# Attention into a mixture of experts on one core: rows of two chunks leave in four transfers of 32 partitions each

## The chip, the core and the metric

The kernel runs on one NeuronCore of a Trainium2 chip. The metric is the device time of one execution in microseconds. A core has a matrix engine (PE, with its weight loads listed as PEld), a vector engine (DVE), a scalar engine (ACT), a general engine (POOL), a queue engine that issues most transfers (SP), and 16 DMA engines that carry them.

## The reference

Eight batches of eight heads go through causal attention with a window of 128 and a linear bias. The result, 4608 rows of 512 numbers, is routed: each row goes to the one of eight experts with the largest gate logit, and its output is scaled with the gate's probability.

```python
scores = scale * np.matmul(q, k.transpose(0, 1, 3, 2))           # q, k, v: (8, 8, 576, 64)
mask = (rel >= 0) & (rel < window)                               # window 128
attn = np.exp(scores - max); attn = attn / (attn.sum(-1) + 1e-9)
x = np.matmul(attn, v).transpose(0, 2, 1, 3).reshape(4608, 512)
logits = x @ w_gate                                              # 8 experts
out[mask] = gate_w[mask, None] * (np.maximum(xe @ w1[e], 0.0) @ w2[e])   # per expert e, F = 1024
```

## The kernel before

**Attention.** The 4608 rows are cut into 36 chunks of 128 (`make_chunks`): per two batches, four chunks of the first, one mixed chunk with the last 64 rows of both ("tail"), and four of the second. Each chunk goes through named steps. `S` are the score matmuls, `F` the masking fold and the row maximum (DVE, L194 and L197), `E` the exponentials (ACT, L203), `T` and `C` turn the probabilities, `P` masks them on POOL, `A` multiplies with v on PE (L242), `X` copies the result, transposed, out of PSUM (ACT, L331), `Y` turns it back into rows on DVE (L334) and calls `store_rows`, which writes the rows to a DRAM buffer `xd`. `I` makes the inverse row sums and stores them beside the rows ("tails", L1322). `G`, `M`, `B`, `L` make the gate logits: PE (L250), a copy on DVE (L350), PE (L257), DVE (L261). The steps `I` and `G` to `L` run once for a batch of one or two chunks (`BATCHES`).

**What sets the order.** A table, `WHEN`, gives each step a time in chunks. During attention the order on all five engines is the one written by hand from this table. Every engine takes its instructions strictly in that order, so an instruction that waits holds up all behind it on its engine.

**Buffers.** `Y` writes into two tiles `x_sb` in turn, one chunk each, so that `Y` of a chunk has to wait until the stores of the chunk two before have landed. `X` writes into `xT`, a tile for two chunks, two such tiles in turn.

**The stores.** `store_rows` issues four transfers for a chunk on SP's queue (L1318). Each takes 32 rows: the source is all 128 partitions of a quarter of `x_sb`, the destination has an outermost dimension of 4 (the quarter of a row), then 32 rows, then 128 numbers (512 bytes). In `xd` a row has four quarters of `SUB` = 128 + `TAIL` numbers, 136 here: 544 bytes.

**SP's queue.** The loads of q (L79, L81), k (L67), v (L90) and the experts' weights (L810, L1060), the row stores, the tails and the gates all stand in this one queue. Its transfers take eight completion counters in turn (`DMAHW0` to `DMAHW7`), and an issue first waits until the transfer that last used its counter, eight places before in the queue, has landed.

**The experts.** From 256 us on, expert by expert, POOL gathers rows of `xd` (L721, L756), they are turned and split into a high and a low part (`xh`, `xl`), and PE runs two layers of three matmuls each on such parts of 4-byte numbers (`first_layer`, L777, and `layer2`, L982). The first 256 rows of the first expert have operands of their own, `e_xh` and `e_xl`, and start while attention still runs.

**Where tiles lie.** Tiles stand one after the other in each partition's memory. By the sizes of the tiles before them, `wh`, `wl` (the split weights), `e_hh`, `e_hl`, `w_raw`, k, q and v start 192 bytes behind a multiple of 512, `xh`, `xl`, `hh` and `hl` 160 bytes behind one, and `e_xh` and `e_xl` on one.

Of the kernel before, what the change touches and what calls it, by code (L numbers as in the profile page):

```python
# [10 lines left out]
F32 = mybir.dt.float32  # L11
# [9 lines left out]
B, H, S, D = 8, 8, 576, 64  # L21
N, DM, E, F = B * S, H * D, 8, 1024
QB = 32
NP = H // 2
GW = 32
TAIL = 8
SUB = 128 + TAIL
# [10 lines left out]
def attention(ctx, tc, st, qT, qE, kT, v, c1, cb, gw, load_c2, logits, chunk_done, store_rows, store_tails, chunks, begun):  # L38
# [5 lines left out]
    ptp = ctx.enter_context(tc.tile_pool(name="a_pt", bufs=2))  # L44
    xp = ctx.enter_context(tc.tile_pool(name="a_x", bufs=2))
    ps_s = ctx.enter_context(tc.tile_pool(name="ps_s", bufs=1, space=PSUM))
# [55 lines left out]
    warm = const.tile([128, 512], BF16, name="warm")  # L102
    nc.vector.memset(warm, 0.0)

    def clear_scores():
# [9 lines left out]

    rows_sb = [const.tile([128, 4, 128], F32, name=f"x_sb{k}") for k in range(2)]
    tails = [const.tile([128, 4, NP * BMAX + TAIL - NP], F32, name=f"tl_sb{k}") for k in range(3)]
# [14 lines left out]
    nc.sync.dma_start(out=c1_sb, in_=c1)  # L132
    first = const.tile([128, 1], F32, name="first")
    nc.vector.memset(first, 0.0)
# [111 lines left out]

    def gates(xT, nb):
        g_ps = ps_r.tile([128, 512], F32, name="g_ps")
        for p in range(NP):
            nc.tensor.matmul(out=g_ps[GW * p:GW * p + GW, 0:128 * nb], lhsT=gw_sb[:, p, :], rhs=xT[:, p, 0:128 * nb],  # L250
                             start=True, stop=True)
        return g_ps

    def turn_gates(lT, nb):
        st["r_ps"] = r_ps = ps_r.tile([128, 512], F32, name="r_ps")
        for j in range(nb):
            nc.tensor.transpose(out=r_ps[:, 128 * j:128 * j + 128], in_=lT[:, 128 * j:128 * j + 128], identity=ident)  # L257
        return r_ps

    def scale_logits(r_ps, tl, dst, nb):  # L260
        nc.vector.tensor_tensor(  # L261
            out=dst.rearrange("q b p c e -> q (b p) c e"),
            in0=r_ps[:, 0:128 * nb].rearrange("q (x y) -> q x y", y=GW)[:, :, 0:2 * E].rearrange("q x (c e) -> q x c e", c=2),
            in1=tl.rearrange("q (c a) x -> q x c a", c=2)[:, 0:NP * nb, :, 0:1].to_broadcast([128, NP * nb, 2, E]), op=ALU.mult)

    ahead = {}
# [27 lines left out]
    def do(op, ch):  # L294
# [33 lines left out]
        elif op == "X":  # L328
            if j == 0:
                tiles["xT", c0] = xp.tile([128, NP, 128 * BMAX], F32, name="xT", bufs=2)  # L330
            nc.scalar.copy(out=every("xT")[:, :, 128 * j:128 * j + 128], in_=tiles.pop(("x", ch)))  # L331
        elif op == "Y":
            rows_sb.append(rows_sb.pop(0))
            keep(tc, nc.vector.transpose(  # L334
                out=rows_sb[-1].rearrange("p s (n j) -> p s n j", j=32),
                in_=every("xT")[:, :, 128 * j:128 * j + 128].rearrange("p n (s i) -> p s n i", i=32)))
            store_rows(ch, subs, rows_sb[-1])
        elif op == "I":
            tails.append(tails.pop(0))
            tl = tiles["inv", c0] = tails[-1]  # L340
            nc.vector.reciprocal(
                out=tl.rearrange("q (c a) x -> q c a x", c=2)[:, :, :, 0:NP * nb],
                in_=every("sum")[:, 0:H * nb].rearrange("q (x c) -> q c x", c=2).unsqueeze(2).to_broadcast([128, 2, 2, NP * nb]))
            for k in range(nb):
                store_tails(c0 + k, chunks[c0 + k], tl[:, :, NP * k:NP * k + TAIL])
        elif op == "G":
            tiles["g", c0] = gates(every("xT"), nb)
        elif op == "M":
            tiles["lT", c0] = lT = xp.tile([128, 128 * BMAX], F32, name="lT", bufs=1)
            nc.vector.tensor_copy(out=lT[:, 0:128 * nb], in_=tiles.pop(("g", c0))[:, 0:128 * nb])  # L350
        elif op == "B":
            tiles["r", c0] = turn_gates(tiles.pop(("lT", c0)), nb)
        elif op == "L":
            scale_logits(tiles.pop(("r", c0)), every("inv"), logits(c0, nb), nb)
            chunk_done(ch)
# [42 lines left out]
    while plan:  # L398
# [21 lines left out]
STAGE = 3  # L420
BMAX = 2
BATCHES = ((0, 2), (2, 2), (4, 1), (5, 2), (7, 2), (9, 1), (10, 2), (12, 2), (14, 1), (15, 2), (17, 2), (19, 2), (21, 2),
           (23, 2), (25, 2), (27, 2), (29, 1), (30, 2), (32, 2), (34, 1), (35, 1))
# [363 lines left out]
def moe_early(ctx, tc, st):  # L787
# [3 lines left out]
    xl = pool.tile([128, 4, EARLY], F32R, name="e_xl")  # L791
    gate = pool.tile([128, 104], F32, name="e_gate")[:, 0:PROF[0]]
    st["np"] = nw_ = ctx.enter_context(tc.tile_pool(name="m_w", bufs=1))
# [48 lines left out]
def moe_static(ctx, tc, st, w12, out):  # L842
# [25 lines left out]

    pace = yp.tile([1, 1], F32, name="pace", bufs=1)

# [410 lines left out]
def attn_moe_kernel(ctx, tc, qT, qE, kT, v, c1, cb, c2, gw, w12, out):  # L1281
# [9 lines left out]
    with ExitStack() as actx:  # L1291
# [21 lines left out]

        def store_rows(ch, subs, x_sb):
            for lo, n, t0 in halves(subs):
                for s in range(n // QB):
                    t = t0 + QB * s
                    nc.sync.dma_start(out=st["xd"][t:t + QB].rearrange("i (a x) -> a i x", a=4)[:, :, 0:128], in_=x_sb[:, lo + s])  # L1318

# [76 lines left out]
```

## Time and profile before

| | |
|---|---|
| median of 3 runs | 701.09 us (700.82 to 707.48) |
| the profiled execution | 703.12 us, of it 701.4 us from the first to the last instruction (the span) |
| busy share of the span | PE 91%, PEld 75%, DVE 60%, ACT 46%, POOL 42% |
[...]
| DMA | 98.28 MB, mean 140 GB/s |

Busy shares are means over two stages with different limits: attention until about 284 us of the span, and the experts from there on. They are read by stage, from the table of windows in the rows below.

### The profile page before, as it was taken

The numbers are of one execution on the slowest core, as the hardware profiler recorded it, in microseconds if no ns is written. First come the engines' busy times: TensorE is split into PE (matmuls) and PEld (weight loads), VectorE is DVE, ScalarE is ACT, GpSimd is POOL, SyncE is SP. The second block draws the span as 40 slices with busy tenths as digits, with TensorE's granted clock in tenths as the row PEclk, the third lists the DMA queues.
The fourth block names the chain that finished last, engine by engine and source line by source line (L and its number), as shares of the span: only waits on it lengthen the run. The fifth ranks groups of instructions, "written<-read, shape, count | busy, mean of one in ns | idle before, by whom it ended". The sixth has DMA issues, their size and how long they took to land.

```text
span 701.4 us, 17994 instructions
## 1 busy us (share of the span) xinstructions
PE 640.5 (91%) x7040; PEld 523.0 (75%) x7041; DVE 420.9 (60%) x979; ACT 319.1 (46%) x963; POOL 292.0 (42%) x391
## 2 busy tenths in 40 slices
PE   7889687787769878999999999999999999999995
PEld 4667565565547566788989888989898888888884
DVE  4557757685667957857366457456547546458411
ACT  6858667767666533144233433433423423424311
POOL 2444535554644321302650762573474362282202
PEclk9989979899889979999999999999999999999999
DMA  7767676667765512643742633543443343354201
GB/s 235 179 195 193 175 197 168 188 172 194 199 169 142 126 33 37 184 141 106 259 154 74 185 107 107 159 119 92 151 132 104 126 143 107 116 158 128 90 1 56
DMA packets 92904, 98.28 MB, mean 140 GB/s; under 512 B 31301, under 2 KB 68165, under 8 KB 92818
## 3 DMA queue, kind: packets, MB, share of 16 engines
q1 hardware_dynamic: 84194, 76.54, 38.9%
q0 software_dynamic: 8336, 20.32, 10.0%
q8 instruction: 56, 0.92, 0.5%
q10 hardware_dynamic: 288, 0.26, 0.1%
q14 instruction: 30, 0.25, 0.1%
HBM read 77.60 MB, written 19.50 MB: 138 GB/s over the span
## 4 chain that ended last, share of the span: by engine, by line
PE 52%; DMA 17%; DVE 10%; issue 10%; SPq 5%; POOL 4%; ACT 2%; POOLq 0%; DVEq 0%; ACTq 0%
PE l_ps L777 23%; PE y_ps L982 22%; DMA xd<-x_sb 12%; SPq L1318 3%; DMA w_raw<-w 2%; POOL xg L756 2%; DVE x_sb L334 2%; DVE nmax L197 1%; DVE s_ps L194 1%; DMA k_sb<-kT 1%; POOL out L970 1%; DMA xd<-tl_sb 1%; PE s_ps L184 1%; ACT pe L203 1%; PE b_ps L242 1%
## 5 line engine op out<-in xcount | busy, mean ns | idle before, releaser
L756 POOL DMA_INDIRECT xg<-xd,od_idx x112 | 116.6, 1041 | 35.3 <-issue 33.9
L784 DVE SCALAR_TENSOR_TENSOR hl<-l_ps,hh 128x320 fp32r<-128x320 f32 (+5 forms) x104 | 52.0, 501 | 126.9 <-ACT hh L780 126.8
L780 ACT ACTIVATE hh<-l_ps 128x320 fp32r<-128x320 f32 (+5 forms) x104 | 46.5, 447 | 176.5 <-PE l_ps L777 176.4
L203 ACT ACTIVATE pe<-s_ps,nmax 128x128 f32<-128x128 f32 x288 | 102.6, 375 | 39.0 <-DVE nmax L197 34.7
L226 POOL TENSOR_SCALAR_AFFINE_SELECT pT<-pT 128x512 f32<-128x512 f32 x112 | 71.6, 661 | 106.9 <-ACT pT L321 106.4
L982 PE MATMUL y_ps<-wh,hh 128*128 128x512 f32 (+5 forms) x280 | 110.7, 395 | 0.0
L982 PE MATMUL y_ps<-wh,hl 128*128 128x512 f32 (+5 forms) x280 | 110.5, 395 | 0.0
L982 PE MATMUL y_ps<-wl,hh 128*128 128x512 f32 (+5 forms) x280 | 110.4, 394 | 0.0
L970 POOL DMA_INDIRECT out<-y,od_pidx x33 | 34.8, 1056 | 151.3 <-ACT y L988 145.0
L1075 DVE TENSOR_TENSOR wl<-w_raw,wh 128x512 fp32r<-128x512 f32 x114 | 74.0, 690 | 30.8 <-ACT wh L1071 30.8
L777 PE MATMUL l_ps<-xh,wh 128*128 128x320 f32 (+8 forms) x416 | 82.1, 318 | 0.7 <-ACT xh L739 0.7
L777 PE MATMUL l_ps<-xh,wl 128*128 128x320 f32 (+8 forms) x416 | 81.3, 317 | 0.0
L777 PE MATMUL l_ps<-xl,wh 128*128 128x320 f32 (+8 forms) x416 | 81.2, 317 | 0.0
L777 PEld LDWEIGHTS l_ps<-xh,wh 128*128 128x128 f32 x416 | 68.2, 188 | 9.6 <-ACT xh L739 1.2
L242 PE MATMUL b_ps<-pT,v_sb 128*64 128x128 f32 (+2 forms) x1152 | 71.2, 277 | 1.2 <-POOL pT L226 0.8
L242 PEld LDWEIGHTS b_ps<-pT,v_sb 128*64 128x64 f32 (+1 forms) x1152 | 61.5, 145 | 10.4 <-issue 5.9
L777 PEld LDWEIGHTS l_ps<-xl,wh 128*128 128x128 f32 x416 | 66.4, 189 | 2.1
L777 PEld LDWEIGHTS l_ps<-xh,wl 128*128 128x128 f32 x416 | 66.2, 189 | 2.1
L184 PE MATMUL s_ps<-k_sb,q_sb 64*32 64x160 f32 (+4 forms) x2304 | 58.9, 313 | 3.6 <-POOL rsum L315 2.8
L982 PEld LDWEIGHTS y_ps<-wh,hl 128*128 128x128 f32 (+5 forms) x280 | 51.2, 183 | 13.9
L203 ACT ACTIVATION_READ_ACCUMULATOR pe<-s_ps,nmax 128x1 f32 x288 | 61.3, 213 | 0.0
L1071 ACT CAST wh<-w_raw 128x1024 fp32r<-128x1024 f32 x57 | 59.4, 1042 | 4.0 <-DMA w_raw<-w 4.0
(221 smaller groups left out, 915.3 us busy)
## 6 DMA issues: line engine op xcount, KB each, us to landing
w_raw<-w SPq DMA_DIRECT2D x56, 512.0 KB
xd<-x_sb SPq DMA_DIRECT2D x144, 64.0 KB
v_sb<-v SPq DMA_DIRECT2D x32, 256.0 KB
q_sb<-qT SPq DMA_DIRECT2D x31, 256.0 KB
k_sb<-kT SPq DMA_DIRECT2D x23, 256.0 KB
w_raw<-w SPq DMA_DIRECT2D x16, 256.0 KB
k_sb<-kT SPq DMA_DIRECT2D x8, 384.0 KB
w_n<-w SPq DMA_DIRECT2D x3, 1024.0 KB
```

Of the source, the lines that this page charges most:

```text
L184: nc.tensor.matmul(out=s_ps[rows(u), c, n, x0:x1], lhsT=blocks["q", b, m][h, 2 * g + n, rows(u % 2 if tail else u)], rhs=batch[b][h, 2 * g ...
L203: nc.scalar.activation(out=pe[:, h, :], in_=s_ps[:, c, n, lo:lo + 128], func=AF.Exp, bias=nmax[:, 2 * c + n:2 * c + n + 1], scale=1.0, acc ...
L226: nc.gpsimd.affine_select(out=part(cut(kb)), in_=part(cut(1)), pattern=pat(sign), base=0, channel_multiplier=-sign, compare_op=op, fill=0.0)
L242: nc.tensor.matmul(out=x_ps[64 * c:64 * c + 64, p, q], lhsT=blocks["v", b, m - 1 + kb][0:kk, D * h:D * h + D], rhs=pT[0:kk, kb, h, q], sta ...
L756: ins = tc.nc.gpsimd.indirect_dma_start(out=g[:, s], out_offset=None, in_=parts, in_offset=bass.IndirectOffsetOnAxis(ap=idx[:, s], axis=0),)
L777: nc.tensor.matmul(out=ps, lhsT=a[:, 128 * d:128 * d + 128], rhs=b[:, d], start=(k == 0), stop=(k == 11))
L780: nc.scalar.activation(out=hh, in_=ps, func=AF.Relu)
L784: nc.vector.scalar_tensor_tensor(out=hl, in0=ps, scalar=0.0, in1=hh.bitcast(F32), op0=ALU.max, op1=ALU.subtract)
L970: ins = nc.gpsimd.indirect_dma_start(**kw).ins
L982: nc.tensor.matmul(out=ys[t][0:n], lhsT=a[:, tl], rhs=b[:, 512:1024], start=(f == 0 and k == 0), stop=(f == 7 and k == 2))
L1071: keep(tc, nc.scalar.copy(out=wh, in_=raw))
L1075: keep(tc, eng.tensor_tensor(out=wl[:, sl], in0=raw[:, sl], in1=wh.bitcast(F32)[:, sl], op=ALU.subtract))
```

## The change

`TAIL` is 5 and not 8: a quarter of a row in `xd` takes 133 numbers, 532 bytes. `x_sb` holds two chunks (eight blocks of 32 rows, two such tiles). `Y` writes its half, and the stores are issued only after the last chunk of a pair (`PAIRS`): four transfers of 32 partitions, one for each quarter of a row, with 32 rows outermost and 512 bytes innermost. Tail chunks keep the old form. Per nine chunks that makes 20 transfers for the rows where there were 36; in the last nine, where chunks 34 and 35 go alone, 24. In place of `xT` stands one tile `xT_sb` with three chunks in a ring. The copy `lT` of the gate logits moves into the tile `warm`, whose zeros only the first warm-up matmuls use. `first`, `e_gate` and `pace` change size or place, so that `wh`, `wl`, `e_hh`, `e_hl`, `xh`, `xl`, `hh`, `hl`, `w_raw`, k, q and v all start on a multiple of 512 bytes.

```diff
-TAIL = 8
+TAIL = 5
 ...
-    rows_sb = [const.tile([128, 4, 128], F32, name=f"x_sb{k}") for k in range(2)]
+    rows_sb = [const.tile([128, 8, 128], F32, name=f"x_sb{k}") for k in range(2)]
+    xT_sb = const.tile([128, 3, NP, 128], F32, name="xT_sb")
 ...
-    first = const.tile([128, 1], F32, name="first")
+    first = const.tile([128, 32], F32, name="first")[:, 0:1]
 ...
-    def gates(xT, nb):
+    def ring(c0, nb):
+        return sorted((ch % 3, ch) for ch in range(c0, c0 + nb))
+
+    def gates(c0, nb):
         g_ps = ps_r.tile([128, 512], F32, name="g_ps")
+        at = [k for k, _ in ring(c0, nb)]
         for p in range(NP):
-            nc.tensor.matmul(out=g_ps[GW * p:GW * p + GW, 0:128 * nb], lhsT=gw_sb[:, p, :], rhs=xT[:, p, 0:128 * nb],
-                             start=True, stop=True)
+            nc.tensor.matmul(out=g_ps[GW * p:GW * p + GW, 0:128 * nb], lhsT=gw_sb[:, p, :],
+                             rhs=xT_sb[:, at[0]:at[-1] + 1:max(1, at[-1] - at[0]), p, :], start=True, stop=True)
         return g_ps
 ...
+    def row_place(ch):
+        c0, n = next((c, n) for c, n in PAIRS if c <= ch < c + n)
+        return n, ch - c0, ch == c0 + n - 1
 ...
         elif op == "X":
-            if j == 0:
-                tiles["xT", c0] = xp.tile([128, NP, 128 * BMAX], F32, name="xT", bufs=2)
-            nc.scalar.copy(out=every("xT")[:, :, 128 * j:128 * j + 128], in_=tiles.pop(("x", ch)))
+            nc.scalar.copy(out=xT_sb[:, ch % 3], in_=tiles.pop(("x", ch)))
         elif op == "Y":
-            rows_sb.append(rows_sb.pop(0))
+            n, i, last = row_place(ch)
+            if i == 0:
+                rows_sb.append(rows_sb.pop(0))
             keep(tc, nc.vector.transpose(
-                out=rows_sb[-1].rearrange("p s (n j) -> p s n j", j=32),
-                in_=every("xT")[:, :, 128 * j:128 * j + 128].rearrange("p n (s i) -> p s n i", i=32)))
-            store_rows(ch, subs, rows_sb[-1])
+                out=rows_sb[-1][:, 4 * i:4 * i + 4].rearrange("p s (n j) -> p s n j", j=32),
+                in_=xT_sb[:, ch % 3].rearrange("p n (s i) -> p s n i", i=32)))
+            if last:
+                store_rows(chunks[ch - i], rows_sb[-1], 4 * n)
 ...
+PAIRS = tuple((9 * s + c, n) for s in range(4) for c, n in ((0, 2), (2, 2), (4, 1), (5, 2), (7, 2 - s // 3)) + ((8, 1),) * (s // 3))
 ...
-    gate = pool.tile([128, 104], F32, name="e_gate")[:, 0:PROF[0]]
+    gate = pool.tile([128, 72], F32, name="e_gate")[:, 0:PROF[0]]
 ...
-    pace = yp.tile([1, 1], F32, name="pace", bufs=1)
+    pace = xgp.tile([1, 48], F32, name="pace", bufs=1)[:, 0:1]
 ...
-        def store_rows(ch, subs, x_sb):
-            for lo, n, t0 in halves(subs):
-                for s in range(n // QB):
-                    t = t0 + QB * s
-                    nc.sync.dma_start(out=st["xd"][t:t + QB].rearrange("i (a x) -> a i x", a=4)[:, :, 0:128], in_=x_sb[:, lo + s])
+        def store_rows(subs, x_sb, n):
+            xd = st["xd"]
+            if subs[0][0] != subs[2][0]:
+                for k, (b, i) in enumerate(subs):
+                    t = b * S + QB * i
+                    nc.sync.dma_start(out=xd[t:t + QB].rearrange("i (a x) -> a i x", a=4)[:, :, 0:128], in_=x_sb[:, k])
+                return
+            t = subs[0][0] * S + QB * subs[0][1]
+            for a in range(4):
+                nc.sync.dma_start(out=xd[t:t + QB * n].rearrange("(s i) (a x) -> a i s x", i=QB, a=4)[a, :, :, 0:128],
+                                  in_=x_sb[QB * a:QB * a + QB, 0:n])
```

On SP's queue, where the rows of chunks 6 and 7 were stored (a row with x4 stands for four instructions; `tl_sb` are the tails, `w_n` and `w_raw` weights), stood before:

```order
L1318 DMA xd<-x_sb_116 4x32x128 x4
L810 DMA w_n<-w 128x512
L90 DMA v_sb<-v 128x512
L81 DMA q_sb<-qT 128x512
L67 DMA k_sb<-kT 128x4x128
L1318 DMA xd<-x_sb_117 4x32x128 x4
L810 DMA w_n<-w 128x512
L90 DMA v_sb<-v 128x512
L81 DMA q_sb<-qT 128x512
L1322 DMA xd<-tl_sb_119 512x1x8 x2
```

The same place with the change, from the store of chunks 5 and 6 together on:

```order
L1334 DMA xd<-x_sb_114 32x8x128 x4
L821 DMA w_n<-w 128x512
L89 DMA v_sb<-v 128x512
L80 DMA q_sb<-qT 128x512
L66 DMA k_sb<-kT 128x4x128
L821 DMA w_n<-w 128x512
L89 DMA v_sb<-v 128x512
L80 DMA q_sb<-qT 128x512
L1339 DMA xd<-tl_sb_117 512x1x5 x2
```

The four stores of chunk 7 are gone from between the loads; they leave with those of chunk 8, five rows later in the queue. The loads keep their order.

On DVE, from `Y` of chunk 8 to `Y` of chunk 9 (STREAM_TRANSPOSE; the brackets name the counters that an instruction waits on, `DMAHW` those of SP's transfers), stood before:

```order
L334 STREAM_TRANSPOSE x_sb_116<-xT 128x512 [waits DMAHW2_49,DMAHW1_49,DMAHW3_49,DMAHW0_49,Activation_49]
L194 COPY_PREDICATED s_ps<-c_sb,s_ps 128x4x128 [waits PE_49]
L197 TENSOR_REDUCE nmax<-s_ps 128x4 [waits DVE_49]
L341 RECIPROCAL tl_sb_120<-rsum 128x4x4 [waits DMAHW5_49,Pool_49]
L573 SCALAR_TENSOR_TENSOR p<-t,rank 128x5
L575 TENSOR_TENSOR lp<-c_sb,p 128x640 [waits DVE_49]
L578 TENSOR_SCALAR c<-mk 128x5
L580 TENSOR_SCALAR big<-rank 128x5
L194 COPY_PREDICATED s_ps<-c_sb,s_ps 128x4x128 [waits PE_49,Activation_49]
L197 TENSOR_REDUCE nmax<-s_ps 128x4 [waits DVE_49]
L334 STREAM_TRANSPOSE x_sb_117<-xT 128x512 [waits DMAHW2_49,DMAHW1_49,DMAHW3_49,DMAHW0_49,Activation_49]
```

With the change:

```order
L344 STREAM_TRANSPOSE x_sb_113<-xT_sb 128x512 [waits Activation_49]
L195 COPY_PREDICATED s_ps<-c_sb,s_ps 128x4x128 [waits PE_49]
L198 TENSOR_REDUCE nmax<-s_ps 128x4 [waits DVE_49]
L352 RECIPROCAL tl_sb_118<-rsum 128x4x4 [waits DMAHW6_49,DMAHW5_49,Pool_49]
L584 SCALAR_TENSOR_TENSOR p<-t,rank 128x5
L586 TENSOR_TENSOR lp<-c_sb,p 128x640 [waits DVE_49]
L589 TENSOR_SCALAR c<-mk 128x5
L591 TENSOR_SCALAR big<-rank 128x5
L195 COPY_PREDICATED s_ps<-c_sb,s_ps 128x4x128 [waits PE_49,Activation_49]
L198 TENSOR_REDUCE nmax<-s_ps 128x4 [waits DVE_49]
L344 STREAM_TRANSPOSE x_sb_114<-xT_sb 128x512 [waits DMAHW6_49,DMAHW5_49,DMAHW7_49,DMAHW4_49,Activation_49]
```

The order is the same; every second `Y` has lost its wait on transfers, and the other waits for the pair two pairs back.

## Rows read from the trace of the kernel before

**Rows 1.** The table of windows: start:end and length, busy us, clock, DMA share, GB/s.

```profile
0.00:46.97 46.97, 39.59 (x890) 26.66 (x899) 22.63 (x49) 30.89 (x132) 17.79 (x43) 0.93 0.74 206
46.97:75.71 28.74, 27.06 (x665) 20.04 (x649) 22.25 (x53) 23.69 (x103) 14.53 (x26) 1.00 0.71 189
75.71:209.20 133.49, 103.72 (x2295) 74.17 (x2289) 89.41 (x195) 90.12 (x362) 66.62 (x101) 0.89 0.69 183
209.20:244.02 34.82, 30.65 (x689) 22.86 (x691) 29.60 (x81) 20.72 (x88) 14.83 (x25) 0.89 0.58 140
284.00:701.40 417.40, 408.48 (x2264) 353.04 (x2262) 229.76 (x494) 141.05 (x238) 170.38 (x186) 1.00 0.41 124
```

**Rows 2.** The chain of waits, 60 to 130 us: start, length, what.

```profile
55.81 6.55 DMA xd<-x_sb
...
62.37 1.09 SPq L1318
...
63.51 0.50 SPq L1318
...
64.06 4.89 DMA xd<-x_sb
...
68.97 6.62 DMA xd<-x_sb
...
75.71 0.71 DVE x_sb L334
```

**Rows 3.** Timeline of DVE at Y of chunks 4, 9, 27 and 32.

```profile
46.97 0.70 DVE L334 STREAM_TRANSPOSE x_sb<-xT 128x512 f32<-128x512 f32 x1
...
75.71 0.71 DVE L334 STREAM_TRANSPOSE x_sb<-xT 128x512 f32<-128x512 f32 x1 [1.36 <-DMA xd<-x_sb]
...
209.20 0.71 DVE L334 STREAM_TRANSPOSE x_sb<-xT 128x512 f32<-128x512 f32 x1 [3.25 <-DMA xd<-x_sb]
...
244.02 0.70 DVE L334 STREAM_TRANSPOSE x_sb<-xT 128x512 f32<-128x512 f32 x1
```

**Rows 4.** Waits, 75.71 to 209.20 us: total us, times, longest.

```profile
POOL pT L226 <- ACT pT L321: 67.7, 24, 7.4
DVE x_sb L334 <- DMA xd<-x_sb: 26.9, 14, 4.8
ACT pe L203 <- DVE nmax L197: 22.1, 24, 2.8
PE r_ps L257 <- DVE lT L350: 19.3, 9, 2.7
DVE x_sb L334 <- DMA xd<-tl_sb: 3.8, 2, 2.4
```

**Rows 5.** Windows of 1 us of loads, and of 1.8 us of row stores alone.

```profile
91.00:92.00 1.00, 1.00 (x16) 0.83 (x16) 0.21 (x1) 0.67 (x4) 0.00 (x1) 1.00 0.99 340
100.50:102.30 1.80, 0.83 (x7) 0.56 (x8) 1.08 (x4) 1.56 (x9) 0.00 (x0) 0.63 0.29 75
```

**Rows 6.** Timeline of SP's queue at the stores of two chunks.

```profile
97.70 3.71 SPq L1318 DMA_DIRECT2D xd<-x_sb  x4
101.45 0.55 SPq L1060 DMA_DIRECT2D w_raw<-w  x1
102.10 0.43 SPq L90 DMA_DIRECT2D v_sb<-v  x1
102.64 0.37 SPq L81 DMA_DIRECT2D q_sb<-qT  x1
103.06 0.62 SPq L67 DMA_DIRECT2D k_sb<-kT  x1
103.77 4.19 SPq L1318 DMA_DIRECT2D xd<-x_sb  x4
```

**Rows 7.** Waits of POOL, 28 to 42 us.

```profile
POOL q_sb L85 <- DMA q_sb<-qT: 7.0, 1, 7.0
```

**Rows 8.** Timeline of PE: first-layer matmuls on the two kinds of operands, then the second layer.

```profile
269.30 0.63 PE L777 MATMUL s_ps<-e_xh,wh 128*128 128x256 f32 x4
269.77 0.63 PE L777 MATMUL s_ps<-e_xh,wl 128*128 128x256 f32 x4
270.25 0.63 PE L777 MATMUL s_ps<-e_xl,wh 128*128 128x256 f32 x4
270.72 0.40 PE L777 MATMUL s_ps<-e_xh,wh 128*128 128x256 f32 x2
...
354.56 0.76 PE L777 MATMUL l_ps<-xh,wh 128*128 128x320 f32 x4
...
356.32 0.39 PE L982 MATMUL y_ps<-wh,hh 128*128 128x512 f32 x1
```

**Rows 9.** The chain of waits in the experts' stage.

```profile
345.59 3.71 PE l_ps L777 x24
349.30 3.49 PE y_ps L982 x15
352.79 3.69 PE l_ps L777 x24
```

More of the change, by code (lines that the diff above doesn't have):

```diff
@@ L44, in attention @@
     ptp = ctx.enter_context(tc.tile_pool(name="a_pt", bufs=2))
-    xp = ctx.enter_context(tc.tile_pool(name="a_x", bufs=2))
     ps_s = ctx.enter_context(tc.tile_pool(name="ps_s", bufs=1, space=PSUM))
@@ L103, in attention @@
     nc.vector.memset(warm, 0.0)
+    lT_sb = warm.bitcast(F32)
     def clear_scores():
@@ L245, in av, with turn_gates @@
                 )
-    def gates(xT, nb):
+    def ring(c0, nb):
+        return sorted((ch % 3, ch) for ch in range(c0, c0 + nb))
+    def gates(c0, nb):
         g_ps = ps_r.tile([128, 512], F32, name="g_ps")
+        at = [k for k, _ in ring(c0, nb)]
         for p in range(NP):
-            nc.tensor.matmul(out=g_ps[GW * p:GW * p + GW, 0:128 * nb], lhsT=gw_sb[:, p, :], rhs=xT[:, p, 0:128 * nb],
-                             start=True, stop=True)
+            nc.tensor.matmul(out=g_ps[GW * p:GW * p + GW, 0:128 * nb], lhsT=gw_sb[:, p, :],
+                             rhs=xT_sb[:, at[0]:at[-1] + 1:max(1, at[-1] - at[0]), p, :], start=True, stop=True)
         return g_ps
-    def turn_gates(lT, nb):
+    def turn_gates(c0, nb):
         st["r_ps"] = r_ps = ps_r.tile([128, 512], F32, name="r_ps")
-        for j in range(nb):
-            nc.tensor.transpose(out=r_ps[:, 128 * j:128 * j + 128], in_=lT[:, 128 * j:128 * j + 128], identity=ident)
+        for n, (_, ch) in enumerate(ring(c0, nb)):
+            j = ch - c0
+            nc.tensor.transpose(out=r_ps[:, 128 * j:128 * j + 128], in_=lT_sb[:, 128 * n:128 * n + 128], identity=ident)
         return r_ps
@@ L346, in do @@
         elif op == "G":
-            tiles["g", c0] = gates(every("xT"), nb)
+            tiles["g", c0] = gates(c0, nb)
         elif op == "M":
-            tiles["lT", c0] = lT = xp.tile([128, 128 * BMAX], F32, name="lT", bufs=1)
-            nc.vector.tensor_copy(out=lT[:, 0:128 * nb], in_=tiles.pop(("g", c0))[:, 0:128 * nb])
+            nc.vector.tensor_copy(out=lT_sb[:, 0:128 * nb], in_=tiles.pop(("g", c0))[:, 0:128 * nb])
         elif op == "B":
-            tiles["r", c0] = turn_gates(tiles.pop(("lT", c0)), nb)
+            tiles["r", c0] = turn_gates(c0, nb)
         elif op == "L":
```

## The prediction

> **What bounds the kernel now.** I read the table of windows first, because two stages stand in the span [rows 1]. From 284 us on PE is busy 408.5 of 417.4 us at full clock: that stage ends when PE ends, and only faster matmuls shorten it. Before that no engine is full. From 75.71 to 209.20 us PE is busy 78%, DVE and ACT 67%, and the clock is granted at 0.89 on average. So waits set the pace there. The chain of waits says which [rows 2]: a store of rows lands, SP issues the next stores, one of those lands, and only then DVE may do `Y`. The chain hangs on the transfers of `x_sb`, 4.9 to 6.6 us each, not on an engine.
>
> The pace itself is read from the starts of `Y` [rows 3]. Chunks 4 to 9 take (75.71 - 46.97) / 5 = 5.75 us each, chunks 9 to 27 (209.20 - 75.71) / 18 = 7.42 us, chunks 27 to 32 (244.02 - 209.20) / 5 = 6.96 us. `Y` waits for transfers in the middle stretch alone, 26.9 + 3.8 = 30.7 us there [rows 4], and 3.25 us at its end [rows 3]: 1.7 us of each chunk's 7.42. The wait for `tl_sb` is the same wait: `Y` reads no tails, it waits on the counters of four row stores. Behind `Y` stand the row maxima and the copy of the gate logits, so ACT's 22.1 us for `nmax` and PE's 19.3 us for `lT` [rows 4] are largely the same time seen from other engines, and are not added.
>
> Why the stores are slow is in two short windows [rows 5]. Where loads run, the 16 DMA engines are busy 0.99 and move 340 GB/s; where only row stores are in flight, 0.29 and 75 GB/s, which is 4.6 of the 16 engines. A chunk's rows are 262,144 bytes: at 75 GB/s they hold those few engines for 3.5 us. All transfers of the stretch are 0.69 x 16 x 7.42 = 82 engine-us a chunk [rows 1]; the rows are 4.6 x 3.5 = 16 of them, and the remaining 66, spread over 16, put 4.1 us on each engine. On the few engines that carry rows this makes 3.5 + 4.1 = 7.6 us a chunk, against a pace of 7.42. These engines are full; the others have a third of their time free.
>
> **The change, part by part.**
>
> *Stores spread out and rarer.* The new transfer has 32 partitions outermost on both sides where the old one had 4 on the side of `xd`. No row shows such a form. Its bounds are the old rate (4.6 engines) and the rate of the loads (all 16); I take the latter, because the loads, whose outermost count is 128, use all, and the form with a 4 uses about four. Then the rows cost every engine 16 / 16 = 1.0 us a chunk, and the transfers' own floor is 82 / 16 = 5.1 us a chunk instead of 7.6.
>
> [...]
>
> *Waits of Y.* In a pair only the first `Y` waits, for stores issued after the second `Y` two pairs back: three chunks earlier, where it was two. Three chunks at 6 us are 18 us; a store lands 4.9 to 6.6 us after its issue [rows 2]. I take all 30.7 + 3.25 us of waits as gone.
>
> *SP's queue.* 60 of 144 row stores go. They cost 3.71 and 4.19 us for four [rows 6], much of it waiting for the transfer eight places before. Loads come up earlier. The place where that counts is the start: POOL waits 7.0 us for one block of q [rows 7], with the scaling of q, the sums and the masks of other chunks behind it. In the old queue the four stores of chunk 0 stood before that load's group. Bounds: nothing, since the load may be late for other reasons, and the 7.0 us; I take 2.5, about one group of four issues less its waits.
>
> *The ring.* `X` of a chunk needs `Y` and `G` of the chunk three before. `G` stands ahead of the chunk's own `A` in PE's order, and `X` waits for that `A` anyway; `Y` is due 2.8 chunks earlier. Nothing is added unless DVE falls behind by that much. PE's `G` reads two pieces instead of one with the same columns: 0. The copy into `warm` has the buffer count that `lT` had: 0.
>
> *Late rows.* The first chunk's rows of a pair leave a chunk later. Only gathers read them. The first gather covers chunks 0 to 26, which end with a pair, and chunks 34 and 35 go alone, so no reader waits longer: 0.
>
> *Aligned operands.* In the first layer the 12 matmuls of 256 columns on `e_xh` and `e_xl`, which already lie on multiples of 512 bytes, take 270.72 - 269.30 = 1.42 us, 118 ns each; those of 320 columns on `xh` and `xl`, 160 bytes off, (356.32 - 354.56) / 12 = 147 ns [rows 8]; those of 512 columns on `wh` and `wl`, 192 off, 3.49 / 15 = 233 ns [rows 9]. The line through the last two, 0.448 ns a column, gives 118 ns at 256. An aligned moving operand sits on the line of the others: 0, with -2 us (half a per cent of the stage, which this cannot exclude) and +2 us as bounds.
>
> *Rows of 532 bytes.* Gathers move 2% fewer bytes and run beside PE's work: 0.
>
> **The sum.** The new pace of the middle stretch decides. Its floor is 5.5 us (a chunk's share of the 103.7 us busy on PE less 5% for a clock that no longer falls), or 5.1 us (DMA), or 5.0 us (DVE's 89.4 us). The best pace seen without these waits is 5.75, with PE busy 94% and DVE 77%; but DVE then had 22.25 / 5 = 4.45 us a chunk to do, and now has 4.97. The other pace without such waits, 6.96, has DVE busy 29.6 / 5 = 5.9 us a chunk. On the line between them, 4.97 us of DVE work gives 6.2. So 18 x (7.42 - 6.2) = 22 us off; with the 2.5 us at the start 24.5. The profiled execution took 703.1 us, which gives 678.6; it lies 2.0 above the median of the runs, so the forecast is **677**.
>
> **Rivals.**
>
> *The pace of the late stretch, 6.96* (0.14). DVE's routing steps and PE's waits for them remain, and the wait moves from `Y` to PE. For it: ACT and PE wait for DVE also where no transfer is late. Against: DVE has a sixth less to do per chunk in the middle. 18 x 0.46 = 8 us: 693.
>
> *The stores don't get quicker* (0.08). If the new form is carried by as few engines as the old, the bytes on those stay, their 7.6 us a chunk stay, and deeper buffers only let the stores queue longer: 701, no change.
>
> *Slower: rows that no longer start at multiples of 32 bytes* (0.04). A piece of 512 bytes now costs 16 engine-us / 512 = 32 ns. A pitch of 532 bytes could make each write slow at both its ends. At 6.2 us the 16 engines have 6.2 x 15.8 = 98 engine-us; 82 are used, so pieces may cost twice as much for nothing. From 102 ns a piece on the transfers need more than today's 7.42 us; at four times, 128 ns, a chunk takes 8.3 us and the kernel 701 + 18 x 0.85 = 716. Nothing in the rows shows such a price.
>
> *Aligned operands speed PE up* (0.08). [...]
>
> **Numbers.** My forecast has 0.66. Its own range, from the pace of 5.75 with 5 us at the start to a pace of 6.6 with nothing there, is 666 to 686. To hold the time 8 times in 10 the range must reach the late pace too: **665 to 695**; left out are no quicker stores, slower and the faster PE, together 0.20. About 1% is what a measurement of this kernel can tell from no change, 694 to 708. Faster by more: 0.66, the 0.08 of the faster PE and a little over half of the 0.14 at 693, **0.82**; within 1%: the rest of that and 0.08, **0.14**; slower **0.04**.
>
> **What would show it.** In the profile after, the windows with row stores alone should have gone or show a DMA share well above 0.29; `Y` should wait under 5 us for transfers in all; the starts of `Y` of chunks 9 and 27 should lie about 112 us apart; the granted clock there should be above 0.89, DMA share about 0.8; the second layer should still take 3.49 us for 15 matmuls. I am wrong if `Y` still waits, if PE's wait for `lT` grows by what `Y` loses, or if the experts' stage changes its length by more than 3 us.

## The result, and the profile after

The changed kernel takes **671.57 us** (median of 4 runs, 669.93 to 674.76) against 702.36 for the kernel before on the same chip: a ratio of 0.956, 95% interval 0.949 to 0.962. The profiled execution took 672.75 us, of it 671.0 in the span; before it was 703.12 and 701.4.

The table of windows answers to [rows 1]. It is cut at `Y` of chunks 9, 27, 32 and 35 of this run, and once at 44.50 us, 0.9 us ahead of `Y` of chunk 4; the columns are those of [rows 1].

```profile
0.00:44.50 44.50, 37.49 (x854) 25.87 (x859) 21.35 (x48) 30.21 (x131) 17.52 (x42) 0.96 0.81 222
44.50:72.45 27.95, 26.91 (x657) 19.12 (x653) 22.96 (x54) 22.98 (x98) 14.04 (x26) 1.00 0.75 179
72.45:184.26 111.81, 96.78 (x2316) 70.66 (x2315) 89.30 (x196) 86.89 (x360) 65.37 (x100) 0.98 0.89 210
184.26:219.25 34.99, 30.67 (x686) 21.75 (x673) 28.56 (x81) 22.68 (x98) 16.24 (x28) 0.90 0.79 167
241.72:671.00 429.28, 419.63 (x2367) 363.99 (x2365) 241.25 (x562) 143.80 (x251) 173.28 (x189) 1.00 0.40 123
```

The middle stretch, 133.49 us before, takes 111.81, or 6.21 us a chunk and not 7.42. PE has 87% of it to do, at a clock of 0.98. DMA was expected at about 0.8 there and stands at 0.89: something in it costs more than before. The last window runs from `Y` of chunk 35 to the end. It took 433.1 us before (268.32 to 701.4) and takes 429.3.

The chain of waits between 90 and 105 us answers to [rows 2]:

```profile
96.30 6.43 DMA xd<-x_sb
...
102.85 0.71 DVE x_sb L344
```

A store still stands in the chain now and then, one as long as before, but where the lines of [rows 2] lead from store to store, here PE and DVE lie between. For all of the stretch from `Y` 9 to 27, the shares of the chain, before and after (the view cuts its lines short):

```profile
by line: DMA xd<-x_sb 35.5%; DMA w_raw<-w 12.1%; SPq L1318 10.5%; DMA xd<-tl_sb 5.9%; DVE x_sb L334 4.3%; DVE nmax L197 4.2%; DVE s_ps L194 3.4%; issue 3.1%; PE s_ps L184 1.9%; PE b_ps L211 1.7%; PE r_ps L257 1.4%; DVE lT L350 1.3%; DVE gat
```

```profile
by line: DMA xd<-x_sb 11.3%; DMA w_raw<-w 8.5%; PE b_ps L243 7.4%; DMA k_sb<-kT 7.1%; ACT pe L204 6.3%; DVE nmax L198 5.6%; DVE s_ps L195 5.3%; PE s_ps L185 5.0%; issue 4.6%; DMA xd<-tl_sb 3.4%; PE b_ps L212 3.1%; SPq L1330 3.1%; PE r_ps L2
```

The four kinds of transfer in the second line still make 30% of the chain, where the three in the first make 53.5%: stores no longer lead it, but transfers have not left it.

The timeline of DVE, at `Y` of chunks 9, 27 and 35, answers to [rows 3]:

```profile
72.45 0.70 DVE L344 STREAM_TRANSPOSE x_sb<-xT_sb 128x512 f32<-128x512 f32 x1
...
184.26 0.71 DVE L344 STREAM_TRANSPOSE x_sb<-xT_sb 128x512 f32<-128x512 f32 x1 [0.22 <-DMA xd<-x_sb]
...
241.72 0.71 DVE L344 STREAM_TRANSPOSE x_sb<-xT_sb 128x512 f32<-128x512 f32 x1
```

The bracket at chunk 27 held 3.25 us before and holds 0.22. The 30.4 us of the two profiled executions divide so: 3.3 up to `Y` 9 (75.71 to 72.45), 21.7 from `Y` 9 to 27, 1.7 from `Y` 27 to 35, 3.8 behind it.

The waits between `Y` 9 and 27 (us in total, times, longest) answer to [rows 4]:

```profile
POOL pT L227 <- ACT pT L331: 46.4, 19, 5.7
ACT pe L204 <- DVE nmax L198: 14.2, 11, 2.6
DVE s_ps L195 <- PE s_ps L185: 10.7, 11, 1.6
...
DVE x_sb L344 <- DMA q_sb<-qE: 2.1, 2, 1.1
PE r_ps L263 <- DVE warm L360: 3.1, 5, 1.0
DVE x_sb L344 <- DMA xd<-x_sb: 0.7, 2, 0.4
DVE x_sb L344 <- ACT xT_sb L339: 0.4, 1, 0.4
```

`Y`'s 30.7 us for transfers have become 2.1 + 0.7, and PE's 19.3 for the gate logits 3.1. The wait for the ring is 0.4. New at the top on DVE is its wait for PE's scores, 10.7 us where it was 3.0: DVE is now often early.

Two microseconds in which only row stores are in flight answer to the second row of [rows 5]:

```profile
74.00:76.00 2.00, 1.53 (x50) 0.89 (x46) 1.44 (x5) 2.00 (x12) 1.32 (x3) 1.00 1.15 289
```

289 GB/s against 75, at a share of 1.15 against 0.29 (above 1, because records of pieces on one engine overlap). So nearly all 16 engines must carry rows now; the trace does not name the engine of a piece.

SP's queue answers to [rows 6]; the row stores of a pair:

```profile
94.59 2.52 SPq L1334 DMA_DIRECT2D xd<-x_sb  x4
```

Four issues for two chunks stand 2.52 us on the queue. In [rows 6] it was 3.71 and 4.19 us for the four of each chunk. Those are long ones, though; over the stretch from `Y` 9 to 27 one issue took (shortest, median and longest, in ns), before and after:

```profile
L1318 SPq DMA_DIRECT2D xd<-x_sb x74: 503/555/1777, 77.4 to 208.7; - x74
```

```profile
L1334 SPq DMA_DIRECT2D xd<-x_sb x32: 302/502/1268, 71.9 to 176.6; - x32
```

A single issue is little shorter; there are about half as many.

The chain of waits in the stage of the experts answers to [rows 9]:

```profile
306.49 3.45 PE y_ps L993 x15
309.94 3.66 PE l_ps L788 x24
```

15 second-layer matmuls take 3.45 us and not 3.49, 24 first-layer ones 3.66 and not 3.69. The first-layer matmuls of 256 columns on `e_xh` and `e_xl` answer to the first rows of [rows 8]; in PE's timeline:

```profile
241.76 0.64 PE L788 MATMUL s_ps<-e_xh,wl 128*128 128x256 f32 x4
...
243.20 0.64 PE L788 MATMUL s_ps<-e_xh,wl 128*128 128x256 f32 x4
```

(243.20 - 241.76) / 12 = 120 ns, 118 before: these have gained nothing.

### The profile page after: what moved, and what is told of

Same layout as the page of the kernel before. It is cut to its first block, busy times and chain, and to the rows that moved or that the text cites. A ratio compares the mean times of both kernels' runs of the same rounds, so it can differ in the third digit from the quotient of the medians.

```text
span 671.0 us, 17895 instructions
## 1 busy us (share of the span) xinstructions
PE 627.7 (94%) x7040; PEld 514.7 (77%) x7041; DVE 418.2 (62%) x979; ACT 315.2 (47%) x963; POOL 291.1 (43%) x391
## 4 chain that ended last, share of the span: by engine, by line
PE 61%; DVE 11%; issue 10%; DMA 9%; ACT 3%; SPq 2%; POOL 2%; POOLq 0%; DVEq 0%; ACTq 0%
PE l_ps L788 25%; PE y_ps L993 24%; DMA xd<-x_sb 3%; PE b_ps L243 3%; ACT pe L204 2%; DVE nmax L198 2%; PE s_ps L185 2%; DVE s_ps L195 2%; DMA k_sb<-kT 2%; DMA xd<-tl_sb 2%; DMA w_raw<-w 1%; PE b_ps L212 1%; DVE x_sb L344 1%; SPq L1334 1%; POOL out L981 1%
## 5 line engine op out<-in xcount | busy, mean ns | idle before, releaser
L243 PE MATMUL b_ps<-pT,v_sb 128*64 128x128 f32 (+2 forms) x1152 | 69.1, 272 | 0.7 <-POOL pT L227 0.7
L243 PEld LDWEIGHTS b_ps<-pT,v_sb 128*64 128x64 f32 (+1 forms) x1152 | 59.4, 141 | 9.5 <-issue 5.5
L204 ACT ACTIVATION_READ_ACCUMULATOR pe<-s_ps,nmax 128x1 f32 x288 | 64.5, 224 | 0.0
```

Of the source, the lines that this page charges most:

```text
L204: nc.scalar.activation(out=pe[:, h, :], in_=s_ps[:, c, n, lo:lo + 128], func=AF.Exp, bias=nmax[:, 2 * c + n:2 * c + n + 1], scale=1.0, acc ...
L243: nc.tensor.matmul(out=x_ps[64 * c:64 * c + 64, p, q], lhsT=blocks["v", b, m - 1 + kb][0:kk, D * h:D * h + D], rhs=pT[0:kk, kb, h, q], sta ...
```

## The experiments

Three questions: is it the form of the stores or the deeper buffers; what shortened the stage of the experts; and why is DMA busier than expected? Times are medians. Ratios are to the kernel before, whose median beside the experiments was 702.3, 703.3 and 703.9 us in the three groups of runs.

### Alignment alone, on the kernel before

```diff
-    gate = pool.tile([128, 104], F32, name="e_gate")[:, 0:PROF[0]]
+    gate = pool.tile([128, 56], F32, name="e_gate")[:, 0:PROF[0]]
 ...
-    pace = yp.tile([1, 1], F32, name="pace", bufs=1)
+    pace = xgp.tile([1, 8], F32, name="pace", bufs=1)[:, 0:1]
```

> The kernel before with only the addresses of the aligned operands changed; stores, buffers and row pitch stay as before. Theory A: alignment alone shortens the matmuls of the experts by about 1% (15 second-layer matmuls in 3.45 us and not 3.49, 24 first-layer ones in 3.66 and not 3.69), and the stage from Y of chunk 35 to the end from 433 to about 429 to 430 us; the time falls by 3 to 4 us, to about 698 against 701 to 702 for the kernel before. Rival A0: addresses do nothing, the experts' stage was shorter for another reason (rows that come earlier, lighter DMA); second layer 3.49 us, time within 1 us of the kernel before. In both, chunks 9 to 27 keep 7.4 us each.

695.14 us, ratio 0.990 (0.988 to 0.992): 7.2 us less. The window from `Y` of chunk 35 to the end, and a stretch of the chain (start, length, what):

```profile
265.59:695.00 429.41, 418.89 (x2367) 363.93 (x2365) 242.27 (x562) 145.20 (x251) 173.95 (x189) 1.00 0.40 123
```

```profile
342.56 3.66 PE l_ps L777 x24
346.23 3.44 PE y_ps L982 x15
```

The stage takes 429.4 us as theory A said, 3.7 less than before, and its matmuls the shorter times; the whole fell by twice what A expected. PE is busy 418.9 us there where a kernel with only the form of the stores changed (below) has 422.3. The other 3 to 4 us lie in attention (chunks 9 to 27 took 130.87 us and not 133.49), with too little between two profiles to say that addresses did it.

### Everything 192 bytes off

```diff
-    gate = pool.tile([128, 72], F32, name="e_gate")[:, 0:PROF[0]]
+    gate = pool.tile([128, 120], F32, name="e_gate")[:, 0:PROF[0]]
```

> The changed kernel with one tile made longer, so that wh, wl, e_hh, e_hl, xh, xl, hh, hl, w_raw, k, q and v all lie 192 bytes behind a multiple of 512; stores, ring and pitch stay. Theory A: second layer back to 3.49 us for 15, time 3 to 4 us above the changed kernel, about 675. Rival A0: no difference, 671 to 672. In both, chunks 9 to 27 keep 6.2 us each.

675.94 us, ratio 0.961 (0.958 to 0.965). That is the time theory A named, but the changed kernel, run again in another group, took 673.73, which is not to be told from it, and the chain of the stage says otherwise:

```profile
342.93 3.66 PE l_ps L788 x24
346.60 3.44 PE y_ps L993 x15
```

The matmuls keep the shorter times, and PE is busy 418.9 us from `Y` of chunk 35 on, as with alignment alone; so theory A was wrong on the boundary: multiples of 512 are not what counts. 192 is a multiple of 64. In the kernel before `wh` and `wl` lay at 192, but `xh`, `xl`, `hh` and `hl` at 160, which isn't one.

### One operand 32 bytes off a multiple of 64

First `xh`, `xl`, `hh`, `hl`, then `wh`, `wl`:

```diff
-    pace = xgp.tile([1, 48], F32, name="pace", bufs=1)[:, 0:1]
+    pace = xgp.tile([1, 88], F32, name="pace", bufs=1)[:, 0:1]
```

```diff
-    first = const.tile([128, 32], F32, name="first")[:, 0:1]
+    first = const.tile([128, 24], F32, name="first")[:, 0:1]
 ...
-    gate = pool.tile([128, 72], F32, name="e_gate")[:, 0:PROF[0]]
+    gate = pool.tile([128, 80], F32, name="e_gate")[:, 0:PROF[0]]
 ...
-    pace = xgp.tile([1, 48], F32, name="pace", bufs=1)[:, 0:1]
+    pace = xgp.tile([1, 40], F32, name="pace", bufs=1)[:, 0:1]
```

> The changed kernel with xh, xl, hh, hl 160 bytes behind a multiple of 512 (32 behind one of 64), as before the change; wh and wl stay on 512. With all of them 192 bytes off the second layer had kept 3.44 us, so multiples of 512 are not what counts. Theory M (a moving operand that is not on a multiple of 64 bytes costs): the first layer, whose moving operand is xh or xl, goes back to 3.69 us for 24, the second stays at 3.44. Theory W (a stationary operand off 64 costs): the second layer, whose stationary operand is hh or hl, goes back to 3.49, the first stays at 3.66. Both back: either role costs. Time 671 to 675 in each.

> The changed kernel with wh and wl (and w_raw, w_n, e_hh, e_hl) 32 bytes behind a multiple of 512; xh, xl, hh, hl stay on 512. Theory M: the second layer, whose moving operand is wh or wl, goes to 3.49 us for 15 or more, the first stays at 3.66. Theory W: the first layer, whose stationary operand is wh or wl, goes to 3.69 for 24, the second stays at 3.44. Time 671 to 675 in each.

677.08 us, ratio 0.962 (0.957 to 0.966), and 676.01, ratio 0.961 (0.958 to 0.965). The chain of the first:

```profile
343.43 3.71 PE l_ps L788 x24
347.13 3.50 PE y_ps L993 x15
```

and of the second:

```profile
339.70 3.69 PE l_ps L788 x24
343.39 3.50 PE y_ps L993 x15
```

Neither theory alone: both layers go back in both kernels. It is enough that one of the two operands, moving or stationary, lies 32 bytes off a multiple of 64, and both off (that was never the case here) was not tried. Four places behind a multiple of 512 were measured, 0 and 192 without the cost and 32 and 160 with it; a boundary of 64 fits them, but no other place was tried. From `Y` of chunk 35 on these kernels take 431.9 and 431.3 us, 2 to 3 more than the changed kernel, and 3.5 to 4 more than its second profile (427.8); their times lie 1 to 2 us above what was expected.

### The form of the stores alone

On the kernel before (tail chunks keep their form):

```diff
-                for s in range(n // QB):
-                    t = t0 + QB * s
-                    nc.sync.dma_start(out=st["xd"][t:t + QB].rearrange("i (a x) -> a i x", a=4)[:, :, 0:128], in_=x_sb[:, lo + s])
 ...
+                for a in range(4):
+                    nc.sync.dma_start(out=st["xd"][t0:t0 + n].rearrange("(s i) (a x) -> a i s x", i=QB, a=4)[a, :, :, 0:128],
+                                      in_=x_sb[QB * a:QB * a + QB])
```

> The kernel before with only the form of the row stores changed: still four a chunk and two tiles of one chunk, but each takes 32 partitions with 32 rows outermost, not 128 partitions with 4 quarters outermost. Theory S (the few engines that carried the rows were full): most of the gain comes from this alone; chunks 9 to 27 at 6.2 to 6.5 us, since a store lands within the two chunks (12 us) that Y gives it; time about 680 to 685. Rival D (buffers and rarer stores made the gain): chunks 9 to 27 stay above 7 us, time above 693.

682.68 us, ratio 0.971 (0.968 to 0.973). Chunks 9 to 27, in the table of windows:

```profile
76.29:193.03 116.74, 98.60 (x2315) 72.32 (x2311) 90.04 (x197) 87.52 (x359) 66.68 (x101) 0.94 0.75 205
```

and the wait that is left to `Y` there:

```profile
DVE x_sb L334 <- DMA xd<-x_sb: 10.8, 7, 2.5
```

6.49 us a chunk: theory S. The form alone brings 20 us; 10.8 us of `Y`'s waits stay, with only one chunk between a store and the `Y` that needs its tile.

### Deep buffers with the old form, at rows of 532 and of 544 bytes

```diff
-            if subs[0][0] != subs[2][0]:
-                for k, (b, i) in enumerate(subs):
+            if True:
+                for k in range(n):
+                    b, i = (subs[k] if subs[0][0] != subs[2][0] else (subs[0][0], subs[0][1] + k))
```

> The changed kernel with only the old form of the row stores: eight a pair, each with the 4 quarters outermost; pairs of chunks, deeper buffers, ring, alignment and pitch stay. Theory S: the few engines that carry rows are full again, a chunk takes 7.4 to 7.6 us between chunks 9 and 27 however deep the buffers; time 690 to 698. Rival D: three chunks of room for a store are enough, pace 6.2 to 6.5, time 671 to 677.

704.25 us, ratio 1.002 (1.000 to 1.004), above what either theory had; the pace, (209.43 - 75.13) / 18 = 7.46 us, is theory S's. The same edit on the kernel with `TAIL` 8 (further below):

> Rows of 544 bytes, operands aligned, ring and pairs of chunks, but the old form of the stores, eight a pair with 4 quarters outermost. With 532 the same kernel took 704. If the pitch costs in the old form what it costs in the new one, some 9 to 10 us, this takes 694 to 696: the time of the kernel with alignment alone (695), so pairs and depth are worth nothing while few engines carry the rows. If 532 costs only where all 16 engines write, it stays at 702 to 705.

698.84 us, ratio 0.993 (0.990 to 0.997), between the two expectations: 532 costs 5 to 6 us in the old form. The waits of this second kernel between `Y` 9 and 27:

```profile
ACT wh L1098 <- DMA w_raw<-w: 33.7, 10, 6.2
...
PE b_ps L212 <- ACT pT L331: 16.7, 9, 3.8
```

its queue on SP (start, length, what), the stores of two pairs:

```profile
76.10 5.23 SPq L1331 DMA_DIRECT2D xd<-x_sb  x8
...
88.74 7.62 SPq L1331 DMA_DIRECT2D xd<-x_sb  x8
```

and the windows inside them:

```profile
78.00:82.00 4.00, 4.00 (x88) 2.99 (x86) 3.90 (x8) 1.37 (x5) 1.97 (x4) 1.00 0.33 81
93.00:97.00 4.00, 3.25 (x86) 2.24 (x85) 0.89 (x2) 3.46 (x17) 4.00 (x7) 1.00 0.33 76
```

While eight old stores are issued, for 5 to 8 us, DMA stands at 0.33 and moves 76 to 81 GB/s: that is the share of about five engines, and the others have nothing to do, since the loads stand behind the stores in the one queue. `Y` no longer waits on them, but ACT does: 33.7 us for a late `w_raw`, and PE behind it for `pT`. The pace stays at (204.21 - 74.15) / 18 = 7.23 us, and in the first kernel at 7.46. Depth alone gave nothing (alignment, which this kernel has too, had come to 695.14 by itself); it moved the wait from `Y` to the loads. What in the form sets the number of engines no run shows: the old one, 128 partitions with 4 outermost on the side of `xd`, stands at shares of 0.29 to 0.33 (4.6 to 5.3 engines), the new one, 32 partitions with 32 outermost, at 1.15, and no other was tried for the rows.

### Rows of 544 bytes a quarter

```diff
-TAIL = 5
+TAIL = 8
 ...
-    first = const.tile([128, 32], F32, name="first")[:, 0:1]
+    first = const.tile([128, 8], F32, name="first")[:, 0:1]
 ...
-    gate = pool.tile([128, 72], F32, name="e_gate")[:, 0:PROF[0]]
+    gate = pool.tile([128, 56], F32, name="e_gate")[:, 0:PROF[0]]
 ...
-    pace = xgp.tile([1, 48], F32, name="pace", bufs=1)[:, 0:1]
+    pace = xgp.tile([1, 8], F32, name="pace", bufs=1)[:, 0:1]
```

> The changed kernel with rows of 544 bytes a quarter again (TAIL 8), pads set so that all aligned operands stay at multiples of 512. Theory P (rows of 532 bytes make the DMA work slower): the DMA share between Y of chunks 9 and 27 falls from 0.89 to about 0.78 at the same pace, as in the kernel with the form alone, whose rows are 544 (0.75); since few waits on transfers are left there, the time falls little, to 666 to 671. Rival P0 (the transfers are slower because two chunks leave at once): DMA share stays at 0.86 to 0.89, time 670 to 673.

> The changed kernel once more, unaltered, on the same chip and beside the others of this group: 670 to 673 us; it is the measure for the kernel with rows of 544 bytes.

**663.39 us**, ratio 0.942 (0.938 to 0.945); the changed kernel beside it 673.73 (670 to 673 was expected), ratio 0.959 (0.955 to 0.962). The kernel with 544 is 10 us faster than the changed one, and 40 us faster than the kernel before. Its window from `Y` 9 to 27:

```profile
68.48:174.79 106.31, 93.93 (x2299) 69.24 (x2303) 89.44 (x196) 86.19 (x359) 65.07 (x99) 1.00 0.85 232
```

5.91 us a chunk at full clock, 232 GB/s at a share of 0.85 where 532 gives 210 at 0.89. (The profiled execution took 660.62 us, 2.8 less than the median.) A single microsecond with only loads in flight doesn't tell the two pitches apart: the changed kernel moves 244 GB/s in one, but the kernel before, which had 340 in the one of [rows 5], moves 238 in two others. First the changed kernel's, then those of the kernel before:

```profile
84.00:85.00 1.00, 1.00 (x44) 0.68 (x28) 1.00 (x3) 1.00 (x4) 0.56 (x2) 1.00 1.06 244
```

```profile
158.00:160.00 2.00, 0.90 (x40) 0.58 (x39) 1.54 (x4) 1.14 (x6) 0.00 (x0) 1.00 1.00 238
```

The mean over the stretch does: the records of pieces of 2048 bytes, which are loads, average 120 ns in the changed kernel (124 in its second profile), 104 in the kernel before and with 544. The whole price shows in the queue's row of the DMA view (packets, MB, share of 16 engines): the kernel before, the form alone, 544, and the changed kernel, each between its `Y` 9 and 27:

```profile
q1 hardware_dynamic: 38777, 24.07, 67.9%
```

```profile
q1 hardware_dynamic: 37398, 23.51, 74.0%
```

```profile
q1 hardware_dynamic: 38809, 24.30, 83.2%
```

```profile
q1 hardware_dynamic: 36375, 23.09, 87.8%
```

Share x 16 x length / MB gives 60, 59, 58 and 68 engine-us for a megabyte. In the two kernels with deep buffers and the old form, with 532 and with 544, the row is

```profile
q1 hardware_dynamic: 37246, 22.56, 67.9%
```

```profile
q1 hardware_dynamic: 37780, 23.41, 66.6%
```

which gives 65 and 59. So the price goes with the 532 bytes, in both forms, and not with two chunks leaving at once: theory P. By size the run differs from what was expected of P: the DMA share is 0.85, not 0.78, at a quicker pace, and more came of it than "little". With 544 the chain of the stretch has almost no transfers left (3.5%, one load; the changed kernel has 30%, 26% in its second profile):

```profile
by line: ACT pe L204 13.6%; PE b_ps L243 9.6%; DVE nmax L198 7.9%; DVE s_ps L195 7.5%; issue 7.4%; PE s_ps L185 6.2%; DVE rr L600 4.1%; PE b_ps L212 3.9%; DMA v_sb<-v 3.5%; PE r_ps L263 3.1%; PE s_ps L176 2.9%; ACT pT L331 2.8%; DVE x_sb L3
```

Why pieces in rows of 532 bytes make the transfers dearer than in rows of 544 no run here shows.

### Short tails in rows of 544 bytes

```diff
-                nc.sync.dma_start(out=st["xd"][t0:t0 + n].rearrange("t (a x) -> t a x", a=4)[:, :, 128:SUB],
-                                  in_=tl[QB * lo:QB * lo + n])
+                nc.sync.dma_start(out=st["xd"][t0:t0 + n].rearrange("t (a x) -> t a x", a=4)[:, :, 128:133],
+                                  in_=tl[QB * lo:QB * lo + n, :, 0:5])
```

This is on the kernel with rows of 544 bytes, with two transfers more on ACT's queue, at the start, that zero the three numbers left.

> The kernel with rows of 544 bytes a quarter and everything aligned, but each tail is written with 20 bytes and not 32; the three numbers left are zeroed once by two transfers on ACT's queue at the start (18,432 pieces, which load the DMA in the first 40 us or so and may cost up to 10 us there). The form of the kernel with 532 is in it by the size of the tails only; rows start at multiples of 32 again. Theory R (row pieces that start off a multiple of 32 bytes made the difference of 10 us): chunks 9 to 27 keep 5.9 us each, pieces of 2048 bytes take 104 ns. Theory T (tail pieces of 20 bytes made it): 6.3 us a chunk, pieces of 2048 bytes at 120 to 125 ns.

691.09 us, ratio 0.981 (0.977 to 0.986). The zeroing cost far more than expected: `Y` 9 starts 27.6 us later than with 32-byte tails. In the middle stretch, the only place that this run was for, the queue's row and the window:

```profile
q1 hardware_dynamic: 38407, 23.99, 80.4%
```

```profile
96.11:206.93 110.82, 96.45 (x2299) 70.54 (x2303) 89.92 (x197) 86.39 (x359) 65.04 (x99) 0.97 0.82 220
```

0.804 x 16 x 110.82 / 23.99 = 59 engine-us a megabyte, as with 32-byte tails, and pieces of 2048 bytes take 105 ns: the tail pieces are not what made 532 dear. What is left is the rows, by the start of a piece or by the pitch; these two were not told apart. The pace, 6.16 us, lies between the two theories. Among the pieces of the chain of this stretch that the view lists, no transfer stands at all, so it isn't transfers that hold this kernel there; its clock is 0.97 in the stretch and not 1.00, PE is busy 96.45 us and not 93.93, and the profiled execution, 697.11 us, is 6 us above the median. So a kernel without dear transfers can take nearly the changed kernel's pace, and how much of that kernel's 6.21 to 6.34 us is the price of its transfers stays open. The 10 us of the medians, 673.73 against 663.39, stand by themselves.

### Form and alignment without pairs

The edits of the first and of the form alone, together, on the kernel before.

> The kernel before with alignment and the new form, nothing else: one chunk a store, two tiles of one chunk, rows of 544 bytes, no ring. If the parts add, the form alone (-20) and alignment (-7, of it 4 in the stage of the experts) give 676 to 679, and the pairs, with the ring, are worth the remaining 13 to 15 us to 663. If alignment helped only where transfers were late, or the form makes pairs needless, it comes out at 680 to 683, or at 664 to 668.

675.79 us, ratio 0.960 (0.956 to 0.964): the parts add. One after the other: alignment 702 to 695, the form to 676, pairs with the ring to 663, and rows of 532 bytes back to 672 to 674. Whether pairs help by the longer time for a store to land or by the fewer issues on SP's queue, no run tells apart.

## Why the prediction was right

It said 677, range 665 to 695, and 671.57 is inside. The main mechanism was right, the size in part by luck: two of its zeros were wrong, and they had opposite signs. Without the price of rows of 532 bytes, which it put at nothing, the time would have been 663.39, below the range.

- **What bounds the stretch.** Right. The few engines that carried rows made the pace; with their form kept, deeper buffers leave 7.23 to 7.46 us a chunk, near the 7.6 worked out. Less right is the picture of full engines beside free ones: the windows of 0.33 show loads held back in SP's queue, and the trace, which doesn't name engines, can't show the full ones. Its clause that the issues wait mostly for the transfer eight places before isn't borne out either. SP's own waits, for all of the stretch before, have

```profile
SPq L1318 <- DMA xd<-x_sb: 2.1, 7, 0.4
```

while four issues stand 3.71 or 4.19 us on the queue [rows 6]. Those two groups are longer than usual, 0.56 us for an issue being the median; why some issues take as much as 1.8 us before and 1.3 after stays open. The 340 GB/s of loads in [rows 5] is a fast microsecond too, as the 238 of another shows; the sum needed only that loads keep all engines busy, and they do in both (0.99 and 1.00).
- **Sixteen engines.** Right: 289 GB/s with stores alone, at a share of 1.15, from transfers of 32 partitions, four of which follow each other within 2.5 us; the old form had 75 at 0.29.
- **Waits of Y.** Right: 3.0 us are left in all (2.1 + 0.7 + 0.22), under 5.
- **The start.** 2.5 us forecast, 3.3 measured. POOL's wait of 7.0 us for one block of q [rows 7] fell to 4.6, by the 2.5 forecast; POOL's timeline at this block, before and after:

```profile
35.93 0.62 POOL L85 TENSOR_SCALAR q_sb<-q_sb 128x512 f32<-128x512 f32 x1 [7.03 <-DMA q_sb<-qT]
```

```profile
34.25 0.62 POOL L84 TENSOR_SCALAR q_sb<-q_sb 128x512 f32<-128x512 f32 x1 [4.56 <-DMA q_sb<-qT]
```

The rest of the 3.3 is no more than two profiles differ by: the changed kernel, profiled again, came to `Y` 9 at 70.76 us, 1.7 us earlier than the first time.

- **The pace of 6.2.** It came out at 6.21, but not by its reason. The line was drawn from DVE's work, 4.97 us a chunk. The kernel with 544 has the same DVE work (89.44 / 18 = 4.97) and a pace of 5.91. What held the changed kernel at 6.2 to 6.3 was in part transfers, 26 to 30% of its chain against 3.5%; what part is open, as the short tails showed. That the line met 6.21 is luck. The best pace seen, 5.75, which the range took as its edge, was nearer to what the stores' form could give.
- **Rows of 532 bytes: 0.** Wrong, 8 to 10 us. The step counted bytes, and the rival beside it held that pieces may cost twice as much for nothing, as 98 engine-us a chunk stood against 82. The transfers together cost 15% more a megabyte (68 engine-us against 59), and a load's piece of 2048 bytes as much more (120 ns against 104): 0.878 x 16 x 6.21 = 87 of 99 engine-us a chunk. By the prediction's count that still leaves room; yet waits for transfers stayed in the chain. Why, no run shows; that transfers come in bursts is a guess.
- **Aligned operands: 0.** Wrong: the stage of the experts got 3.8 us shorter, outside the bounds of 2 and the 3 that the text took for a sign of being wrong (2.5 to 3.8 by the pairs of profiles that differ in it). The line through 320 and 512 columns met the 118 ns of the aligned 256, but both its points carried the cost, and 1% of 118 ns is less than the rows resolve; and the boundary that it looked at, 512, wasn't the one. The 24 and 15 matmuls of [rows 9] summed over the stage are where 0.03 and 0.04 us count. The chance of 0.08 for a faster PE came from an estimate that no run shows; the runs showed about 1%, 3.44 and 3.66 us and not 3.49 and 3.69.
- **After chunk 27: 0.** 1.7 us to `Y` of chunk 35, within what two profiles differ by: the changed kernel, profiled again, took 58.6 us there, with 59.1 before and 57.5 first.
- **The ring and late rows: 0.** Nothing speaks against it (0.4 us of waits), but the ring was not taken out by itself.

## What to carry to other kernels

Read the DMA share and the GB/s of a short window in which one kind of transfer runs alone: a share far under 1 says how few engines carry it. Here the form of the transfer was then what to change (0.29 with 4 outermost, 1.15 with 32), before deeper buffers, which only moved the wait to the loads behind in the queue (33.7 us of ACT's). One such microsecond is not enough to compare two kernels by: take the mean over a stretch. Check where rows in DRAM start and where matmul operands lie, in the running kernel: rows of 532 bytes against 544 cost 8 to 10 us here, operands 160 bytes behind a multiple of 512 against 0 or 192 some 2 to 4. When a forecast holds, take its parts apart all the same; two errors of opposite sign can make the right sum.

## What the runs showed of the hardware that was not expected

- Row pieces in DRAM with a pitch of 532 bytes made the hardware queue's transfers of the stretch dearer, 68 engine-us a megabyte against 58 to 60 with 544 (65 against 59 in the old form of the stores). Whether the pitch or the start of a piece does it was not tried.
- A matmul operand of 4-byte numbers 32 bytes off a multiple of 64, in either role, cost 1 to 2%: 3.50 us and not 3.44 for 15 of 512 columns, 3.69 to 3.71 and not 3.66 for 24 of 320. At 192 bytes behind a multiple of 512 there was no cost.
- Eight stores in the old form stood 5.23 to 7.62 us on SP's queue, with DMA at 0.33, about five engines' worth, and the loads waited behind them.
